# Reordering the first output block of a retention + MoE kernel: one chunk's casts ahead of two decays, transposes ahead of half units, weight sums and four down steps earlier

## The chip, the cores and the metric

The kernel runs on one core of a Trainium2 chip. A core has a matrix engine (PE in the profile, with its weight loads shown apart as PEld), a vector engine (DVE), a scalar engine (ACT), a general engine (POOL) and a sync engine (SP) that here only issues DMAs. Each engine takes its own instructions in order and waits on semaphores for the others. The metric is the device time of one execution in microseconds. Before the change it is 301.66 us, the median of three runs (300.08, 302.08 and 301.66 us).

## What is computed

Two operations, one behind the other. The first is a retention layer over 8 batches, 8 heads, 576 positions and 64 columns per head: scores of queries and keys, masked to the past and damped by a power of each head's gamma, times the values. Its result, brought to 4608 tokens by 512 columns, goes through a two-layer MLP with a hard-swish between the layers.

```
scores = scale * np.matmul(q, k.transpose(0, 1, 3, 2))
gamma = 1.0 - 2.0 ** (-5.0 - np.arange(H, dtype=np.float32))
Dmat = np.where(rel >= 0, gamma[:, None, None] ** rel[None, :, :], 0.0)
x = np.matmul(scores * Dmat[None], v)              # (B, H, S, D)
x = x.transpose(0, 2, 1, 3).reshape(B * S, H * D)  # 4608 x 512
h = x @ w_in                                       # 512 -> 2048
g = h * np.clip(h + 3.0, 0.0, 6.0) / 6.0
out = g @ w_out                                    # 2048 -> 512
```

The inputs and the output are fp32 in DRAM; the kernel's matrix products take fp16.

## The kernel before, in words

**Blocks and chunks.** The 4608 tokens are taken as nine blocks of 512. Block 0 holds the first 64 positions of all eight batches (the "heads" functions); block kb from 1 to 8 holds the last 512 positions of batch kb-1, in four chunks of 128 positions, numbered c = 4 kb to 4 kb + 3. So chunks 4 to 7 belong to block 1, 8 to 11 to block 2, and so on. A running state carries the past from chunk to chunk.

**Steps of a chunk.** Each step has a letter in the written-out plans:

- `c` (`casts`, line 182): keys to fp16 (ACT; POOL for chunks 7 to 9), for an even chunk the queries of two chunks, scaled, in two halves (`L192`, both on POOL, but for chunks 4 and 6 the second half on DVE), the values scaled (`L195`, POOL). It also issues the loads of a later chunk on SP.
- `t` (`transposes`, 198): products with an identity on PE into PSUM tiles `ptk` and `ptq`, copied out by ACT (`kT`) and DVE (`qT`), line 211.
- `a` (`scores`, 244) and `s` (`states`, 288): products of keys and queries, and of keys and values, into the two PSUM tiles `pa`; DVE multiplies the scores with the mask (`L267`).
- `u` (`add`, 311): DVE adds the new state (`L314`, and `L317` for the next chunk), POOL damps it (`L318`). `z` (`past`, 320): ACT casts the states to fp16 (`L324` to `L327`).
- `x` (`cross_over`, 347) and `i` (`inner`, 351): products of queries with states, and of scores with values, into the PSUM tiles `po`; `i` first has PE wait for the end of `x`. ACT copies `po` into the block's `xT` (`L370`).

**The MLP.** A unit (`U`, `up_steps`, 492) makes 128 of the 2048 hidden columns for 512 tokens: eight products, `ph`, then ACT's `u` (`L511`) and DVE's `g` (`L513`). A half unit pair (`up_two`, 526; written `L2` or `R2`, for the left or right 256 tokens) makes two such columns groups for half of the tokens with 16 products, one `L539` on ACT and one `L540` on DVE; an `L4` is two pairs. A down step (`D`, `down_plain`, 562) is one product of two halves with `w_out`, 64 steps for a block, into the PSUM tiles `pd`; ACT copies each finished `pd` out (`L574`). Blocks 2 to 8 use `down_strassen` (580), which needs eight sums of quarters of `w_out`, each 128x1024 in fp16 on DVE. `weight_sums` (662) only queues them; each `+1` in a plan emits the next of the queue (`side_sums`, 543, at `L545`). Their targets `ws1` to `ws4` hold other things at first: `ws1` the keys and `ws4` the values of block 0.

**The decays of block 0.** `head_states(c)` (`h` in the plan, 272) computes for c = 0 to 3 the state that the first 64 positions of batches c and c + 4 leave, in two PSUM tiles `pu`, and stores both times a power of gamma in `zh[c]` and `zh[c + 4]`: the first by DVE straight out of PSUM (`L283`), the second by an ACT copy (`L282`) and a POOL multiplication in place (`L284`). `zh[0]` is the past of chunk 4, the others serve later blocks.

**Order.** The order on PE, DVE, ACT, POOL and SP is the order in which the program emits the instructions: nothing rearranges them. It is written by hand as strings, one item a step, which `go` (710) reads from left to right. Three calls of `go` cover block 0's down steps, block 1 and the beginning of block 2; from there a loop with tables sets the order.

**Buffers.** All PSUM tiles but `pd` share a ring of six (`psum`, tag "pp", line 62): each new tile waits until the tile six places before it has been read out. `pd` has a ring of two of its own. Loads of keys and values have four buffers each, of queries two.

Of the kernel before, what the change touches and what calls it, by code (L numbers as in the profile page):

```python
# [16 lines left out]
ALU = mybir.AluOpType  # L17
# [4 lines left out]
def kernel(  # L22
# [9 lines left out]
    nc = tc.nc  # L32
    B, H, S, D = q.shape
# [7 lines left out]
    NCB = BLK // P  # L41
# [45 lines left out]
    zh = [const.tile([P, NP, D], FP32, name=f"zh{b}") for b in range(B)]  # L87
# [184 lines left out]
    def head_states(c):  # L272
        pu = [psum.tile([P, NP, D], FP32, tag="pp", name=f"pu{e}_{c}") for e in range(2)]
        todo = ([], [])
        for i in range(NP):
            for a in range(2):
                j, h2 = divmod(i + NP * a, 2)
                for e in range(2):
                    todo[e].append(mm(pu[e][rows(a), i], kn[rows(e), j, c, h2 * D:h2 * D + D],
                                      vh[rows(e), c, j, h2, :], start=True, stop=True))  # L280
        in_turn(todo)
        nc.scalar.copy(zh[c + NCB], pu[1])  # L282
        nc.vector.tensor_tensor(zh[c], pu[0], decay, ALU.mult)  # L283
        nc.gpsimd.tensor_tensor(zh[c + NCB], zh[c + NCB], decay, ALU.mult)  # L284

    zs, z16s, sums = {}, {}, {}

# [274 lines left out]
    def down_plain(kb):  # L562
        pieces = [range(4 * pc, 4 * pc + 4) for pc in range(4)]
        o = [out_tile(kb, m2) for m2 in range(2)]
        for m2 in range(2):
            pd = [psum.tile([P, DM], FP32, tag="st", bufs=2, name=f"pd{kb}_{2 * m2 + m}") for m in range(2)]
            for fcs in (pieces[0], pieces[2], pieces[1], pieces[3]):
                for m in range(2):
                    for fc in fcs:
                        hf, jq, jr = fc // JH, fc % JH // JQ, fc % JQ  # L570
                        product(pd[m], gt[kb, jq][0][:, hf, m2, jr, P * m:P * m + P], wout16[:, fc, :],
                                start=(fc == 0), stop=(fc == NFC - 1))
                        if fc == NFC - 1:
                            nc.scalar.copy(o[m2][:, m, :], pd[m])  # L574
                            if m:
                                kept.append((kb, m2, o[m2]))
                        yield
# [129 lines left out]
                {"c": cast, "t": lambda c: transposes(c, True, "kq" if c < PE_T else "k" if c < PE_K else ""), "a": scores, "s": states, "u": add, "z": past,  # L707
                 "x": cross_over, "i": inner, "k": keys_heads, "h": head_states, "o": lambda _: store(*kept.popleft())}[what](c)

    def go(plan, kb=None, down=None):  # L710


        units = dict(L=0, R=0, U=0)
        for item in plan.split():
            what, n = item[0], int(item[1:])
            if what == "D":
                for _ in range(n):
                    next(down, None)
            elif what in "LR":
                assert n % 2 == 0  # L720
                for _ in range(n // 2):
                    up_two(kb, units[what], "LR".index(what))
                    units[what] += 2
            elif what in units:
                for _ in range(n):
                    u = units[what] + (units["L"] if what == "U" else 0)
                    up_unit(kb, u, dict(L=0, R=1, U=None)[what])
                    units[what] += 1
            else:
                do([(what, n)])  # L730
        assert units["L"] == units["R"] and units["L"] + units["U"] == (0 if kb is None else NFC)
# [14 lines left out]
    with tc.manual_schedule(engines={ENG.PE, ENG.DVE, ENG.Pool, ENG.Activation, ENG.SP}):  # L746
        sp, act, pool = nc.sync, nc.scalar, nc.gpsimd
        on_act, on_dve = nc.scalar.copy, nc.vector.tensor_copy
        indices()
        for nm in ("k", "q"):  # L750
            landed = load_half(0, nm, 0, sp)
            keys = landed if nm == "k" else keys
            load_half(0, nm, 1, act)
        nc.scalar.activation(warm, half, ACTF.Exp)
        load_half(1, "q", 0, sp)
        load_half(1, "q", 1, act)
        for i in (2, 3):
            for e in range(2):
                load_half(i, "q", e, sp, keys)
        for i in (1, 2, 3):  # L760
            for e in range(2):
                load_half(i, "k", e, pool, None if i == 1 else keys)
            if i == 1:
                nc.gpsimd.memset(pick, 0.0)  # L764
        for i in range(NP):
            load_values(i)
        win_piece(0, 2)
        for n in (1, 2, 3):
            win_piece(n)
        wout = [wout_piece(pc) for pc in (0, 2, 1, 3)]  # L770
        distances()
        idle_products(5)
        mask_of_heads(0)
        cast_heads(0, "k", on_dve)
        picks()
        turn_heads(0, "k", on_act)
        mask_of_heads(1)
        idle_products(4)
        cast_heads(0, "q", on_dve)
        mask_of_heads(2)  # L780
        turn_heads(0, "q", on_act)
        cast_heads(1, "q", on_dve)
        turn_heads(1, "k", on_act)
        turn_heads(1, "q", on_act)
        cast_heads(2, "q", on_dve)
        scores_heads(0)
        mask_of_heads(3)
        idle_products(1)
        turn_heads(2, "k", on_act)
        turn_heads(2, "q", on_act)  # L790
        cast_heads(3, "q", on_dve)
        scores_heads(1)
        idle_products(1)
        turn_heads(3, "k", on_act)
        turn_heads(3, "q", on_act)
        scores_heads(2)
        values_heads(0, on_act)
        scores_heads(3)
        values_heads(1, on_act)
        inner_heads(0, on_act)  # L800
        values_heads(2, on_dve)
        inner_heads(1, on_dve)
        values_heads(3, on_act)
        inner_heads(2, on_dve)
        first = [up_steps(0, u) for u in range(4)]
        for dmc in range(3):
            for unit in first:
                next(unit)
            if dmc == 1:
                inner_heads(3, on_act)  # L810
        for unit in first:
            for _ in unit:
                pass
        decays()
        mask_of_chunk()
        decays_of_chunk()
        fetch(8, wout[0])
        for u in range(4, NFC):
            up_unit(0, u)
        weight_sums(3)  # L820
        weight_sums(1, 2, 4)
        down = down_plain(0)
        go("k0 D4 k1 D4 +1 k2 D4 +1 k3 D5 h0 h1 D4 h2 h3 c4 D7 t4 c5 D7 a4 s4 u4 D3 t5 D3 z4 x4 a5 s5 i4 u5 z5 c6 D7 "
           "x5 i5 D5 L2 t6 c7 L4 a6 s6 u6 L2 t7 z6 L2 x6 a7 s7 i6 u7 z7 D5 L2 c8 x7 i7 t8 D6 "
           "R4 c9 R2 a8 s8 u8 R2 t9 z8 R4 c10 x8 a9 s9 i8 u9 U1 z9 c11 t10 U3",
           1, down)
        down = down_plain(1)
        go("c12 D6 x9 a10 s10 i9 u10 z10 D2 t11 c13 +1 D7 x10 a11 s11 i10 u11 z11 c14 +2 D8 x11 D2 i11 t12 +1 D3 +1 D3 "
           "a12 s12 u12 t13 D2 c15 D2 z12 +1 D4 x12 a13 s13 i12 u13 z13 D1",
           down=down)  # L830
        go("U1 D3 t14 U1 D2 U1 U1 D2 x13 a14 s14 i13 u14 z14 o1 c16 U1 D2 U1 D2 t15 U1 D2 U1 D2 +1 U1 x14 a15 s15 i14 u15 z15 "
           "c17 D2 U1 D2 +1 U1 D2 +1 U1 D2 x15 +1 U1 i15 t16 c18 +1 U1 D2 t17 U1 U1",
           2, down)
        for kb in range(2, NB):
            for _ in down:
                pass
            plain = kb < FIRST
            down = down_plain(kb) if plain else down_strassen(kb)
            per = 4 if plain else 7
            table = FIRST_STEADY if kb == 2 else STEADY  # L840
            c = NCB * (kb + 2)
            owed = 0
            for u in range(NFC):
                if u == 0:
                    owed += per - 2
                    for _ in range(per - 2):
                        next(down, None)
                if kb + 1 < NB:
                    up_unit(kb + 1, u)
                else:  # L850
                    side_sums(1)
                owed -= per
                while owed < 0:
                    next(down, None)
                    owed += 1
                for w, i in table.get(u, []):
                    if w == "D":
                        for _ in range(i):
                            next(down, None)
                        owed += i  # L860
                    else:
                        do([(w, i if w == "+" else c + i)])
        for _ in down:
            pass
# [30 lines left out]
```

## Time and profile before

The profiled execution took 300.3 us, of which the profile's span is 298.6 us; its time lies 1.4 us under the median of the runs. The granted clock of PE is 1.00 throughout.

| | before |
|---|---|
| median of three runs | 301.66 us |
| profiled execution | 300.3 us |
| its span | 298.6 us |
| PE busy | 286.0 us (96%) |
| DVE busy | 215.6 us (72%) |
| ACT busy | 191.1 us (64%) |
| POOL busy | 134.0 us (45%) |
| DMA | 160 GB/s mean |

The times in a profile's lines are microseconds from the start of the span. In a timeline, a line gives start, length, engine, source line, operation, the tile written and the tiles read, the count, and in brackets how long the engine sat idle before it and what released it; an `L` number is a line of the kernel. A matmul's end is modelled and lies past the start of the next one, so the distance between starts tells better how long PE needed for a step than the lengths do. Waits of an engine that nobody waits for cost nothing.

### The profile page before, as it was taken

The page shows a single profiled execution, that of the slowest core. Times are in us where ns is not written, and L with a number is a line of the kernel's source. Part 1 is how long each engine was busy: PE and PEld are TensorE (multiplying, and loading weights), DVE is VectorE, ACT ScalarE, POOL GpSimd, SP SyncE. Part 2 cuts the span into 40 slices and gives each one's busy share as a digit, 9 for nine tenths or more (in the row PEclk, how much of TensorE's full clock was granted, in tenths as well). Part 3 has the DMA queues.
Part 4 walks back from the last instruction along what each step waited for, and adds up shares of the span by engine and source line. Part 5 has one row for each costly group of instructions (what it writes and reads, how often), then busy time and mean ns, then how long its engine had stood idle before and what let it go on. Part 6 is the DMA issues. An engine that isn't in the chain of part 4 may idle for free.

```text
span 298.6 us, 12625 instructions
## 1 busy us (share of the span) xinstructions
PE 286.0 (96%) x5574; PEld 221.2 (74%) x5574; DVE 215.6 (72%) x378; ACT 191.1 (64%) x345; POOL 134.0 (45%) x171
## 2 busy tenths in 40 slices
PE   4999989899999999999999999999999999999995
PEld 2676645778656667878987878878778978778894
DVE  7748554759897668788967797688769776647654
ACT  3748855678866796686676577657766574555420
POOL 8971074455861920729632962386247003100510
PEclk9999999999999999999999999999999999999999
DMA  7999999996999999996999999999906100200114
GB/s 166 151 182 213 233 239 221 232 221 121 164 214 162 207 240 195 186 234 195 218 239 218 172 199 214 148 180 242 149 4 143 74 4 32 102 10 2 72 72 141
DMA packets 119542, 47.86 MB, mean 160 GB/s; under 512 B 92352, under 2 KB 114880, under 8 KB 119488
## 3 DMA queue, kind: packets, MB, share of 16 engines
q1 hardware_dynamic: 114336, 41.56, 70.5%
q0 software_dynamic: 4720, 5.11, 10.5%
q8 instruction: 43, 0.70, 1.0%
q10 hardware_dynamic: 432, 0.39, 0.5%
q14 instruction: 11, 0.09, 0.1%
HBM read 36.70 MB, written 9.44 MB: 155 GB/s over the span
## 4 chain that ended last, share of the span: by engine, by line
PE 84%; POOL 5%; ACT 3%; DMA 3%; DVE 2%; issue 1%; POOLq 0%; ACTq 0%
PE ph L153 39%; PE pm L153 29%; PE pd L153 8%; PE po L232 4%; DMA win<-in_moe_w_in_dram 3%; PE pa L232 2%; POOL hv L440 1%; ACT u L539 1%; DVE g L540 1%; POOL hk L400 1%; PE pu L232 1%; POOL zh L284 1%; ACT kT L211 1%; POOL ws L764 1%; PE ptk L153 1%
## 5 line engine op out<-in xcount | busy, mean ns | idle before, releaser
L153 PE MATMUL ph<-xT,win 128*64 128x512 f16 (+1 forms) x1248 | 144.5, 364 | 0.7 <-DMA win<-in_moe_w_in_dram 0.4
L513 DVE SCALAR_TENSOR_TENSOR g<-u,ph 128x512 f16<-128x512 f32 x132 | 89.5, 685 | 47.7 <-ACT u L511 47.3
L511 ACT ACTIVATE u<-ph,half 128x512 f32<-128x512 f32 x132 | 90.2, 691 | 42.0 <-PE ph L153 39.9
L153 PEld LDWEIGHTS <-win 128*64 128x64 f16 x1248 | 84.2, 136 | 26.4 <-DMA win<-in_moe_w_in_dram 0.9
L153 PEld LDWEIGHTS <-g 128*64 128x64 f16 x928 | 51.8, 110 | 14.8 <-issue 0.6
L153 PEld LDWEIGHTS <-s 128*64 128x64 f16 x896 | 50.2, 110 | 8.1 <-issue 0.2
L318 POOL TENSOR_TENSOR z<-z,gpow 128x256 f32<-128x256 f32 x24 | 16.1, 673 | 70.7 <-DVE z L317 50.0
L153 PE MATMUL pm<-ws,s 128*64 128x256 f16 x672 | 45.4, 273 | 0.0
L195 POOL TENSOR_TENSOR v<-fv,dec 128x512 f16<-128x512 f32 x32 | 35.5, 1112 | 3.0 <-DMA fv<-in_v_dram 3.0
L370 ACT CAST xT<-po 128x256 f16<-128x256 f32 (+1 forms) x44 | 22.6, 585 | 21.4 <-PE po L232 21.4
L609 POOL TENSOR_TENSOR u<-u,p 128x512 f32<-128x512 f32 x7 | 8.9, 1273 | 60.1 <-ACT u L649 53.9
L192 POOL TENSOR_TENSOR q<-fq,dec 128x512 f16<-128x512 f32 x30 | 34.7, 1176 | 0.0
L153 PE MATMUL pd<-wout,g 128*64 128x512 f16 x256 | 33.6, 381 | 0.1
L153 PE MATMUL pm<-wout,g 128*64 128x256 f16 x448 | 31.6, 273 | 0.0
L267 DVE TENSOR_TENSOR a<-pa,mask 128x256 f16<-128x256 f32 (+1 forms) x44 | 21.9, 539 | 8.3 <-PE pa L232 5.1
L545 DVE TENSOR_TENSOR s<-g 128x1024 f16<-128x1024 f16 x28 | 19.3, 692 | 0.2
L324 ACT CAST z<-z 128x512 f16<-128x512 f32 x24 | 14.9, 622 | 5.8 <-DVE z L314 5.5
L188 ACT CAST k<-fk 128x512 f16<-128x512 f32 x29 | 18.0, 622 | 0.1
L153 PE MATMUL pm<-ws,g 128*64 128x256 f16 x224 | 16.7, 274 | 0.0
L153 PE MATMUL pm<-wout,s 128*64 128x256 f16 x224 | 16.4, 273 | 0.1
L232 PE MATMUL po<-qT,z 64*64 64x64 f16 x512 | 12.6, 198 | 2.0 <-ACT z L327 0.9
L232 PEld LDWEIGHTS <-z 64*64 64x64 f16 x512 | 8.0, 105 | 8.0 <-ACT z L324 2.2
(110 smaller groups left out, 293.6 us busy)
## 6 DMA issues: line engine op xcount, KB each, us to landing
fk<-in_k_dram SPq DMA_DIRECT2D x32, 256.0 KB, 4.7
fq<-in_q_dram SPq DMA_DIRECT2D x16, 512.0 KB, 5.9
fv<-in_v_dram SPq DMA_DIRECT2D x32, 256.0 KB, 5.5
out_dram<-o SPq DMA_DIRECT2D x14, 512.0 KB, 3.7
wout<-in_moe_w_out_dram POOLq DMA_DIRECT2D x4, 512.0 KB, 17.8
out_dram<-o SPq DMA_DIRECT2D x7, 256.0 KB, 4.0
win<-in_moe_w_in_dram POOLq DMA_DIRECT2D x3, 512.0 KB, 11.3
hq<-in_q_dram SPq DMA_DIRECT2D x6, 128.0 KB, 4.3
```

Of the source, the lines that this page charges most:

```text
L153: nc.tensor.matmul(out[r], lhs[:, r], rhs, skip_group_check=True, **flags)
L188: (nc.gpsimd.tensor_copy if c in K_POOL else nc.scalar.copy)(by_head(k16), in_rows(st[c]["fk"]))
L192: (nc.vector if e and c in Q_DVE else nc.gpsimd).tensor_tensor(by_head(q16[:, e]), in_rows(st[c]["fq"][:, :, e, :]), in_rows(dd[:, 2 + e, ...
L195: nc.gpsimd.tensor_tensor(v16, st[c]["fv"], dd[:, 1, H:2 * H, :], ALU.mult)
L232: return lambda: nc.tensor.matmul(*args, skip_group_check=True, **flags)
L267: nc.vector.tensor_tensor(a16[:, a, 0:n].rearrange("p x i q -> p (x i) q"), pa[a].rearrange("p x i q -> p (x i) q"), m, ALU.mult)
L318: nc.gpsimd.tensor_tensor(new, new, decay, ALU.mult)
L324: nc.scalar.copy(z16, zs[c])
L370: nc.scalar.copy(xt[:, s], po[s].rearrange("p x n (e r) -> p x n e r", e=2))
L511: nc.scalar.activation(uu[:, 0:n], ph[:, 0:n], ACTF.Relu, bias=half, scale=1.0 / 6.0)
L513: nc.vector.scalar_tensor_tensor(out=g[:, hf, ths, jr, :], in0=by_half(uu), scalar=1.0, in1=by_half(ph), op0=ALU.min, op1=ALU.mult)
L545: nc.vector.tensor_tensor(*pend.popleft())
```

## The change

Four pieces, all between block 0's down steps and the last chunk of block 3.

1. In `head_states`, for c = 0 and 1, DVE multiplies the second state too, straight out of PSUM; the ACT copy and the POOL multiplication stay for c = 2 and 3 only. In the plan `c4` moves ahead of `h2 h3`, so that chunk 4's casts stand ahead of two of the decays on ACT, POOL and DVE.
2. `t6` moves ahead of the first half units (`L2` goes behind it, into a later `L4`), and down steps are placed differently: one more ahead of `t4`, two more ahead of `x4`, two between `x5` and `i5`, one between `x7` and `i7`, fewer behind.
3. Of the six sums that stood in the second plan, four are emitted in the first, between `c5` and `c6`.
4. Block 1's down steps get a generator `ahead` from the start, and the new letter `E` takes four of them ahead of the first full unit `U1`; the second plan starts with two down steps where it had six.

On SP the order is the same as before, on PE no product is added or dropped, DVE gets two instructions more, ACT and POOL two fewer.

```
     def head_states(c):
...
-        nc.scalar.copy(zh[c + NCB], pu[1])
         nc.vector.tensor_tensor(zh[c], pu[0], decay, ALU.mult)
-        nc.gpsimd.tensor_tensor(zh[c + NCB], zh[c + NCB], decay, ALU.mult)
+        if c < 2:
+            nc.vector.tensor_tensor(zh[c + NCB], pu[1], decay, ALU.mult)
+        else:
+            nc.scalar.copy(zh[c + NCB], pu[1])
+            nc.gpsimd.tensor_tensor(zh[c + NCB], zh[c + NCB], decay, ALU.mult)
...
-    def go(plan, kb=None, down=None):
+    def go(plan, kb=None, down=None, ahead=None):
...
-            if what == "D":
+            if what in "DE":
                 for _ in range(n):
-                    next(down, None)
+                    next(down if what == "D" else ahead, None)
...
-        down = down_plain(0)
-        go("k0 D4 k1 D4 +1 k2 D4 +1 k3 D5 h0 h1 D4 h2 h3 c4 D7 t4 c5 D7 a4 s4 u4 D3 t5 D3 z4 x4 a5 s5 i4 u5 z5 c6 D7 "
-           "x5 i5 D5 L2 t6 c7 L4 a6 s6 u6 L2 t7 z6 L2 x6 a7 s7 i6 u7 z7 D5 L2 c8 x7 i7 t8 D6 "
-           "R4 c9 R2 a8 s8 u8 R2 t9 z8 R4 c10 x8 a9 s9 i8 u9 U1 z9 c11 t10 U3",
-           1, down)
-        down = down_plain(1)
-        go("c12 D6 x9 a10 s10 i9 u10 z10 D2 t11 c13 +1 D7 x10 a11 s11 i10 u11 z11 c14 +2 D8 x11 D2 i11 t12 +1 D3 +1 D3 "
-           "a12 s12 u12 t13 D2 c15 D2 z12 +1 D4 x12 a13 s13 i12 u13 z13 D1",
+        down, ahead = down_plain(0), down_plain(1)
+        go("k0 D4 k1 D4 +1 k2 D4 +1 k3 D5 h0 h1 D4 c4 h2 h3 D8 t4 c5 +1 D7 a4 s4 u4 +1 D3 t5 D5 z4 x4 a5 s5 i4 u5 z5 +1 c6 +1 D7 "
+           "x5 D2 i5 D4 t6 c7 L4 a6 s6 u6 L2 t7 z6 L4 x6 a7 s7 i6 u7 z7 D3 L2 c8 x7 D1 i7 t8 D3 "
+           "R4 c9 R2 a8 s8 u8 R2 t9 z8 R4 c10 x8 a9 s9 i8 u9 E4 U1 z9 c11 t10 U3",
+           1, down, ahead)
+        down = ahead
+        go("c12 D2 x9 a10 s10 i9 u10 z10 D2 t11 c13 +1 D7 x10 a11 s11 i10 u11 z11 c14 +1 D8 x11 D2 i11 t12 D6 "
+           "a12 s12 u12 t13 D2 c15 D2 z12 D4 x12 a13 s13 i12 u13 z13 D1",
            down=down)
```

## Prediction

> **What bounds the kernel.** I read the busy times first, then the same by stretches of the span, then in the stretches where PE is not full its timeline, its waits and the chain that ended last. PE has 96% of the span:
>
> ```profile
> PE 286.0 (96%) x5574; PEld 221.2 (74%) x5574; DVE 215.6 (72%) x378; ACT 191.1 (64%) x345; POOL 134.0 (45%) x171
> ```
>
> By stretches (start:end and length, then busy time of PE, its weight loads, DVE, ACT and POOL, the granted clock, the DMA share and GB/s):
>
> ```profile
> 33.00:44.80 11.80, 10.35 (x200) 5.91 (x197) 6.27 (x11) 7.91 (x18) 5.77 (x7) 1.00 1.03 242
> 44.80:52.00 7.20, 6.49 (x180) 3.80 (x180) 3.62 (x9) 3.85 (x9) 2.87 (x4) 1.00 1.11 216
> 52.00:64.30 12.30, 11.03 (x292) 9.11 (x290) 8.77 (x17) 8.63 (x16) 8.02 (x10) 1.00 1.00 222
> ...
> 113.00:282.00 169.00, 168.92 (x3320) 138.20 (x3318) 127.59 (x208) 109.83 (x188) 69.53 (x65) 1.00 0.73 142
> ```
>
> From 113 to 282 us PE is busy 168.92 of 169.00 us, so whatever PE gains ahead of it moves the end one for one; nothing there is touched. The change lies where PE is short of work, 33 to 64 us. The chain of 40 to 44 us shows why at the worst place:
>
> ```profile
> 39.44 0.80 POOL zh L284 x2
> ...
> 40.55 1.05 POOL zh L284
> 41.60 1.01 POOL q L192
> 42.61 0.04 issue
> 42.66 0.64 PE ptq L153 x16
> ```
>
> Four decays run on POOL, then chunk 4's query cast, and PE's transposes wait for that cast. PE's timeline, by starts:
>
> ```profile
> 39.28 1.70 PE L153 MATMUL pd<-wout,g 128*64 128x512 f16 x14
> 40.81 0.39 PE L153 MATMUL ptk<-ident,k 128*64 128x128 f16 x8
> 42.66 0.64 PE L153 MATMUL ptq<-ident,q 128*64 128x128 f16 x16 [1.46 <-POOL q L192]
> ...
> 47.46 0.26 PE L232 MATMUL po<-qT,z 64*64 64x64 f16 x8 [0.64 <-ACT z L327]
> ...
> 55.48 0.32 PE L232 MATMUL pa<-qT,kT 64*64 64x64 f16 x16 [0.34 <-DVE qT L211]
> ...
> 58.73 0.26 PE L232 MATMUL po<-qT,z 64*64 64x64 f16 x8 [0.68 <-DVE g L540]
> ```
>
> A down step costs 0.216 us (seven, 14 products, take 39.28 to 40.79), a half unit pair 0.87 (51.68 to 52.55), a key transpose 0.23 (46.01 less 45.78), a query transpose 0.44 (52.78 to 53.21). Start to start less this work leaves these stalls: 0.12 at `h2`; 1.63 at `t4` (42.66 less 41.03); 0.80 at `x4`; 0.20 at `x5`; 0.35 between `x5` and `i5`; 0.50 at `a6` (54.97 to 55.48); 0.85 at `x6`; 0.35 at `x7`; 0.25 between `x7` and `i7`; and 0.10 changing over at `a4`. Sum **5.15 us**. Behind it, `U1` at 71.68 loses 0.43 (`i8` ends at 71.25) and `x12` at 88.57 loses 0.78.
>
> **The change, step by step.** PE's work is the same, so the sum is the stalls of before less those left. I carry PE, DVE, ACT and POOL through the new order with the durations above.
>
> *Chunk 4's casts.* The decays of `h0` and `h1` go to DVE: two more at 0.41 (four took 1.64), so DVE is done with them at 38.38 + 1.64 = 40.02, as before with its own four. The second `pu` of `h0` is now freed at 39.20, and the ring of six makes `h3` wait for it: 0.15. The two ACT copies saved (0.33 each) lay beside idle ACT and give nothing. The query cast cannot start before its load: DVE's half began at 40.20, released by the load. So POOL starts 1.4 earlier than 41.57, at 40.2. But now both halves start together, with the next decays of DVE behind its half. Alone a POOL half is 1.04; the longest in the trace is 1.49, and DVE's two took 0.68 and 0.93. The casts end between 41.2 and 41.85, against 42.61. With the eighth down step PE reaches `ptq` at 41.37 (39.42 + 8 x 0.216 + 0.22). The second half of `ptq` also needs the ring place of `h2`, freed when DVE has done that decay, 0.41 behind its cast. Stall left: 0.15 to 0.9; I take 0.55, nearer the contended rows. Left at this place 0.12 + 0.15 + 0.55 = 0.82 of 1.75.
>
> *Down steps at `x4`.* The cast of the state was late because `t5`'s copy and two casts (0.58, 0.41, 0.41) follow on ACT. `D5` covers 0.43 more; 0.1 is left of 0.80.
>
> *Sums.* Four sums of 0.69 come into DVE between 43 and 51 us, where DVE idled 0.82, 1.27 and 3.28 us: they fit, alone. They read SBUF beside POOL's casts, and there the trace shows them dear (DVE's lines, then POOL's):
>
> ```profile
> 81.83 2.68 DVE L545 TENSOR_TENSOR ws<-wout,ws 128x1024 f16<-128x1024 f16 x2
> 84.43 1.53 DVE L545 TENSOR_TENSOR ws<-wout 128x1024 f16<-128x1024 f16 x1
> ```
>
> ```profile
> 81.47 2.49 POOL L192 TENSOR_TENSOR q<-fq,dec 128x512 f16<-128x512 f32 x2
> 83.92 1.49 POOL L195 TENSOR_TENSOR v<-fv,dec 128x512 f16<-128x512 f32 x1
> ```
>
> A sum beside POOL takes 1.34 to 1.53 and POOL's cast 1.25 to 1.49. So each may hold DVE 0.69 to 1.53. The first ends ahead of `a4`'s masks or 0.6 into them, which `D3 t5 D5` (1.96) covers; the second and POOL's 0.99 damping put `x5` off: I leave 0.2 there, between 0 and 0.4. The third and fourth stand around chunk 6's query cast: DVE's half would be done by 50.1, POOL's between 49.7 and 51.2, PE at `ptq` at 50.7: 0 to 0.55 left, I take 0.3. Their old places, 81.8 to 88, were no gain: `x12` there waits for ACT's row of `kT`, `o`, `k` and two `z` casts behind `t13`, whose order stays. I leave its 0.78.
>
> The Trainium skill, "SBUF — State Buffer", "Who interferes with whom", says that a vector instruction with two SBUF inputs and a GpSimd one that reads SBUF exclude each other, and the later to start waits for the whole of the other. The 1.53 beside 1.49 agrees; this speaks against pieces 1 and 3, as it makes the two halves of chunk 4's cast follow one another. By that rule at its worst (0.9, 0.4 and 0.55 left at `t4`, `x5` and `t6`) the gain of the sum below would be 2.2 instead of 3.0; without any contention (0.15, 0 and 0) it would be 3.9.
>
> *`D2` and `D1`* between `x` and `i` cover the change of PSUM writer that cost 0.35 and 0.25; nothing of it is left, as 0.43 is over 0.35 and 0.22 near 0.25.
>
> *`t6` ahead of `L4`.* The copies of `qT` (1.28 on DVE) then run beside 1.74 of half units, so `a6` loses its 0.50. `L4` in place of `L2` ahead of `x6` gives ACT and DVE 0.87 more, and the 0.85 falls to 0.15 (the third `g` frees `a7`'s place). But the two pairs put their `u` and `g` ahead of chunk 7's masks. From the end of the first `L4` (taken as 0): its last `u` and `g` end at 1.66, masks and states of chunk 6 at 3.1, three more `g` at 5.2, masks and `L314` of chunk 7 at 6.25, ACT's cast at 6.85; PE has work for 5.95. So `x7` stalls **0.9** where it stalled 0.35. Here between 0.3 and 1.5, as one `g` (0.61) more or less comes ahead.
>
> *`E4`* covers `U1`'s 0.43 with 0.86 of work. What it takes away are four down steps ahead of `x9`, whose state is cast at 74.0, 3.3 us early, and whose ring places are free by 77.53; `x10` then stands about 0.1 ahead of its state. Cost 0.1. No wait is added on SP.
>
> *Loads.* Chunks 4 to 7 land from 40 to 51 us; POOL's waits there are for DVE. From 44 to 64 us DMA moves 216 to 222 GB/s, near the most of any slice (242), but from 70 to 77 us it rests (0.55 of its time, one idle gap of SP from 67 to 72), so chunks from 12 on have room to move forward with PE.
>
> **Sum.** Left: 0.82, 0.1 (`x4`), 0.2, 0, 0.3 (`t6`), 0, 0.15, 0.9, 0, with 0.03 of changing over = 2.5. Gain 5.15 - 2.5 + 0.43 - 0.1 = **3.0 us**, 300.3 - 3.0 = 297.3 for an execution like the profiled one, 298.7 counted from the median of 301.66. The runs spread over both, so I say **297.9**. A change under about 1% (3.0 us) can hardly be told from none here.
>
> **Rivals.**
> - *Every stall goes:* the chain to `x7` is shorter than my sum and the casts do not collide. For it: DVE idles 7.4 us between 41 and 54 us. Gain 5.15 + 0.43 = 5.6, less the load's bound (0.15): 5.4, 2.4 more than the forecast, so 295.5. Against: the load at 40.2 and three `g` ahead of chunk 7. Chance 0.12.
> - *A new wait takes the gain:* PE comes early to `t4`, `t6` and `x7` and finds the upper ends: 0.35, 0.25 and 0.6 more, `x5` 0.2 more, 1.4 in all, and up to 1 us at loads or at the ring. Gain 0.6 to 1.6, some 1.9 less than the forecast: 299.8. That a plan's pieces give each other's gain back (or that the order does nothing at all) ends here too. Chance 0.18.
> - *Slower: DVE starves beside POOL.* If DVE's half of chunk 4's cast had to wait for POOL's whole row `q v zh zh v` (3 x 1.04 + 2 x 0.61 = 4.3), it would end at 45.2 and `ptq`, after the decay behind, at 45.7: 3.9 over my 41.8. The same at chunk 6 (row `z q v k v`, 4.3, against 1.4 allowed) costs 2.9 more: 297.3 + 6.8 = 304.1. It decides once DVE loses to more than about two POOL instructions in a row. Against: from 81.47 to 84.5 both engines moved in turn. Chance 0.10, a fifth of it within 1%.
>
> **Chances and range.** Forecast 0.60, two thirds of it over 3.0 us, as fewer collisions than I took are likelier than more once the four sums fall into DVE's idle time. Faster by over 1%: 0.40 + 0.12 = 0.52. Within: 0.20 + 0.18 + 0.02 = 0.40. Slower: 0.08. The forecast's own range is 296.4 to 299.4; 8 in 10 reaches from the first rival to most of the second: 295.3 to 300.8.
>
> **What would show it.** POOL's `q` starting near 40.2 and PE's `ptq` near 41.5 to 42; the wait of `ptq` for POOL under 0.9; sums of 0.7 to 1.5 us between 43 and 52; no wait at `a6`; `x7` waiting for ACT about 0.9; PE's first right half unit at 61 to 62 in place of 64.32; `U1` without a wait. I am wrong if `ptq` starts past 42.5, if `x7`'s wait is over 1.5, or if loads show among PE's or ACT's waits ahead of 70 us.

## The result, and the profile after

Over fourteen executions each, the changed kernel takes 299.23 us in the median (298.64 to 301.09) and the kernel before 300.9 us (299.33 to 303.17). The ratio is 0.9949, with a 95% interval of 0.9926 to 0.9973: about 1.5 us gained, between 0.8 and 2.2 us (the medians alone lie 1.7 apart). I had forecast 3.0 us and 297.9 us. The direction was right, and the size is half of what I said, so the gain fell among the cases within 1%, not into the likeliest one. That 299.23 still lies inside the forecast's range (296.4 to 299.4), 0.2 us from its end, owes something to luck: single executions of one kernel differ by more, and the gain itself was mis-sized by half.

The profiled execution of the changed kernel took 301.1 us, the longest of its fourteen, with a span of 299.4 us against 298.6 before. From line 284 on, a line of the kernel before has a number higher by 3 in the changed kernel (`L324`, `L327`, `L370`, `L540` and `L545` are now `L327`, `L330`, `L373`, `L543` and `L548`); `decays_pool` keeps the numbers of before. The busy times by stretches after (start:end and length; busy time of PE, its loads, DVE, ACT, POOL; clock; DMA share; GB/s):

```profile
33.00:44.80 11.80, 11.63 (x204) 6.84 (x200) 7.62 (x16) 8.22 (x18) 3.41 (x4) 1.00 0.93 218
44.80:52.00 7.20, 6.98 (x182) 3.75 (x180) 6.39 (x13) 3.86 (x10) 4.65 (x5) 1.00 1.00 225
52.00:64.30 12.30, 11.48 (x298) 9.51 (x296) 9.48 (x18) 8.62 (x17) 9.15 (x11) 1.00 1.08 240
113.00:282.00 169.00, 167.67 (x3302) 136.62 (x3298) 127.09 (x207) 108.59 (x185) 68.70 (x65) 1.00 0.75 141
```

In the three stretches that the change touches, PE's idle time fell from 1.45, 0.71 and 1.27 us to 0.17, 0.22 and 0.82 (roughly the same work: this execution is there about 1 us later). But from 113 to 282 us, where nothing was changed, PE stood idle 1.33 us against 0.08 before. The waits of PE after (line, what it waited for, us in total, times, longest) name two of the losses outside the change:

```profile
PE ph L153 <- DMA win<-in_moe_w_in_dram: 1.5, 2, 1.0
PE po L232 <- issue: 1.0, 1, 1.0
```

The first is at the start, where the loads of `w_in` landed late (0.4 us before); the second is at 153 us and is released by nothing that the profile shows. So the two spans can't be set against each other. I compare marks instead: **L**, where DVE starts its half of chunk 4's query cast (released by the load); chunk 4's `ptq` on PE; **B**, the first right half unit of block 1; **C**, block 2's first full unit. PE does the same work between L and C in both kernels. Before, L to C is 49.30 us, in a second execution 49.23; after, 47.49 and 47.49. That is a gain of **1.8 us**, and it agrees with the timed 0.8 to 2.2. The two ends, DVE's line at L and PE's at C, before and then after:

```profile
40.20 0.93 DVE L192 TENSOR_TENSOR q<-fq,dec 128x512 f16<-128x512 f32 x1 [0.18 <-DMA fq<-in_q_dram]
...
89.50 1.03 PE L153 MATMUL ph<-xT,win 128*64 128x512 f16 x8
```

```profile
41.25 0.69 DVE L192 TENSOR_TENSOR q<-fq,dec 128x512 f16<-128x512 f32 x1 [0.30 <-DMA fq<-in_q_dram]
...
88.74 1.03 PE L153 MATMUL ph<-xT,win 128*64 128x512 f16 x8
```

Counting from L takes the landing of the load as given. L lies 2.66 and 2.63 us behind the first `pu` products in the two profiles of before, 2.49 and 3.07 in the two of after, and 1.76 to 4.37 in the experiments below. Whether the change itself moves the load, so few executions can't tell.

The remaining 0.8 us that the profiled span is longer is a head 1.05 longer and a tail behind C 1.56 longer (210.66 against 209.10), less this gain.

The chain after, at the place where four decays and the cast had stood on POOL:

```profile
31.80 9.42 DMA fq<-in_q_dram
...
41.39 1.46 POOL q L192
```

The decays are gone from it: ahead of the cast now stands chunk 4's query load. PE's timeline after:

```profile
42.89 0.64 PE L153 MATMUL ptq<-ident,q 128*64 128x128 f16 x16 [0.17 <-POOL q L192]
...
46.24 1.25 PE L153 MATMUL pd<-wout,g 128*64 128x512 f16 x10
47.70 0.25 PE L232 MATMUL po<-qT,z 64*64 64x64 f16 x8 [0.21 <-ACT z L330]
...
50.07 0.26 PE L232 MATMUL po<-qT,z 64*64 64x64 f16 x8
50.26 0.62 PE L153 MATMUL pd<-wout,g 128*64 128x512 f16 x4
50.81 0.25 PE L232 MATMUL po<-qT,z 64*64 64x64 f16 x8
50.90 0.30 PE L232 MATMUL po<-a,v 64*64 64x64 f16 x16
...
52.94 1.91 PE L153 MATMUL ph<-xT,win 128*64 128x256 f16 x32
54.79 0.32 PE L232 MATMUL pa<-qT,kT 64*64 64x64 f16 x16
...
59.67 1.26 PE L153 MATMUL ph<-xT,win 128*64 128x256 f16 x16
61.65 0.25 PE L232 MATMUL po<-qT,z 64*64 64x64 f16 x8 [0.72 <-ACT z L327]
...
63.83 2.35 PE L153 MATMUL ph<-xT,win 128*64 128x256 f16 x40
```

The stall at `ptq` is nearly gone, `a6` (54.79) has lost its wait, and `x7` (61.65) is now the dear place: the pair ahead of it needs 0.87, so PE stood 1.11 us from 60.54 on.

### The profile page after: what moved, and what is told of

It is laid out like the page before. It is cut to its first block, busy times and chain, and to the rows that moved or that the text cites. A ratio compares the mean times of both kernels' runs of the same rounds, so it can differ in the third digit from the quotient of the medians.

```text
span 299.4 us, 12624 instructions
## 1 busy us (share of the span) xinstructions
PE 287.2 (96%) x5574; PEld 219.8 (73%) x5574; DVE 216.0 (72%) x380; ACT 190.5 (64%) x343; POOL 133.9 (45%) x169
## 4 chain that ended last, share of the span: by engine, by line
PE 77%; DMA 10%; POOL 6%; ACT 3%; DVE 2%; issue 1%; SPq 0%; POOLq 0%; ACTq 0%
PE ph L153 36%; PE pm L153 29%; DMA wout<-in_moe_w_out_dram 5%; PE pd L153 4%; PE po L232 3%; DMA fq<-in_q_dram 3%; PE pa L232 2%; DMA fv<-in_v_dram 2%; POOL hv L443 1%; POOL hk L403 1%; POOL win L679 1%; PE pu L232 1%; POOL q L192 1%; ACT z L327 1%; ACT kT L211 1%
## 5 line engine op out<-in xcount | busy, mean ns | idle before, releaser
L153 PEld LDWEIGHTS <-win 128*64 128x64 f16 x1248 | 83.1, 136 | 28.4 <-DMA win<-in_moe_w_in_dram 2.1
L153 PEld LDWEIGHTS <-g 128*64 128x64 f16 x928 | 50.6, 110 | 15.5 <-issue 0.4
L153 PEld LDWEIGHTS <-s 128*64 128x64 f16 x896 | 51.0, 110 | 8.2 <-issue 1.1
L153 PE MATMUL pm<-ws,s 128*64 128x256 f16 x672 | 46.1, 273 | 0.2 <-issue 0.2
L192 POOL TENSOR_TENSOR q<-fq,dec 128x512 f16<-128x512 f32 x30 | 35.6, 1204 | 17.2 <-DMA fq<-in_q_dram 17.2
L195 POOL TENSOR_TENSOR v<-fv,dec 128x512 f16<-128x512 f32 x32 | 36.2, 1134 | 2.6 <-PE ph L153 2.6
L373 ACT CAST xT<-po 128x256 f16<-128x256 f32 (+1 forms) x44 | 22.6, 585 | 21.4 <-PE po L232 21.4
L153 PE MATMUL pd<-wout,g 128*64 128x512 f16 x256 | 34.2, 382 | 0.1
L153 PE MATMUL pm<-wout,g 128*64 128x256 f16 x448 | 30.8, 273 | 0.0
L548 DVE TENSOR_TENSOR s<-g 128x1024 f16<-128x1024 f16 x28 | 19.4, 694 | 0.2
L327 ACT CAST z<-z 128x512 f16<-128x512 f32 x24 | 14.9, 620 | 7.0 <-DVE z L317 6.6
```

The costliest lines, as they stand in the source:

```text
L153: nc.tensor.matmul(out[r], lhs[:, r], rhs, skip_group_check=True, **flags)
L192: (nc.vector if e and c in Q_DVE else nc.gpsimd).tensor_tensor(by_head(q16[:, e]), in_rows(st[c]["fq"][:, :, e, :]), in_rows(dd[:, 2 + e, ...
L195: nc.gpsimd.tensor_tensor(v16, st[c]["fv"], dd[:, 1, H:2 * H, :], ALU.mult)
L327: nc.scalar.copy(z16, zs[c])
L373: nc.scalar.copy(xt[:, s], po[s].rearrange("p x n (e r) -> p x n e r", e=2))
L548: nc.vector.tensor_tensor(*pend.popleft())
```

## The experiments

All marks in microseconds. The kernel before has one down step (0.22) fewer ahead of `ptq` and one more behind it; the table counts it ahead in every run, so 0.22 is taken from `ptq` to B and the gain at `ptq` reads 1.04 for 0.82. At `i8`, in some executions, PE stood 0.1 to 0.55 us by the distance of the starts (where the profile names a releaser, it is "issue"); this is taken out of B to C, and 0.72 inside `x5` out of `casts_alone`.

| kernel | L to `ptq` | `ptq` to B | B to C |
|---|---|---|---|
| before, two executions | 2.46, 2.48 (+0.22) | 21.44, 21.34 | 25.18, 25.19 |
| after, two executions | 1.64, 1.65 | 20.94, 20.92 | 24.91, 24.92 |
| `casts_alone` | 1.65 (+0.22) | 21.44 | 25.20 |
| `sums_back` | 1.66 | 20.67 | 24.92 |
| `no_ahead` | 1.65 | 20.93 | 25.19 |
| `units_back` | 1.65 | 21.39 | 24.91 |
| `no_split` | 1.65 | 20.95 | 24.90 |
| `four_ahead_x7` | 1.95 | 20.93 | 24.96 |
| `decays_pool` | 1.65 | 22.60 | 24.90 |
| `pair_after_z7` | 1.65 | 21.04 | 24.94 |
| `z12_early` | 1.95 | 20.91 | 24.72 |
| `casts6_early` | 1.65 | 21.59 | 24.55 |

Marks of kernels with the same order between two marks agree to 0.1 (most to 0.05), while single times of one kernel lie up to 4 us apart. So the verdicts below go by marks, and by times only where many executions were made. Each experiment but `casts_alone` and `casts6_early` is a single execution. The first four expectations count from A, the first `pu` products, and so take in how late the load lands. By those marks two of them look like misses: in `units_back` the load came 3.76 behind A, and `casts_alone` takes 26.89 from A to B and 52.09 from A to C, no less than before (26.78 and 51.96). The later expectations count from L.

**`casts_alone`: the first piece alone, in the kernel before.** `head_states` as after, and

```
-h0 h1 D4 h2 h3 c4 D7 t4
+h0 h1 D4 c4 h2 h3 D7 t4
```

> The kernel before with piece 1 alone: chunk 4's casts ahead of h2 and h3, and DVE taking both decays for the first two chunks; plans otherwise as before. Marks are read from PE's timeline: A is the start of block 0's first state products (pu), B the first right half unit of block 1, C block 2's first full unit. Before: A to B 26.78, A to C 51.96 us; after: 25.08 and 49.99. Theory: the casts alone are worth most of the change, the wait of 1.63 at ptq falls to 0.4 to 0.6 and nothing later takes it back: A to B 25.6 to 25.9, A to C 50.7 to 51.1, time about 0.3 to 0.4% under before. Rival: the next wait (the state cast ahead of x4, 0.80) takes it: A to B 26.3 or more.

Ten executions took 300.48 us in the median against 301.63 of the kernel before: ratio 0.9959, 0.9925 to 0.9992, so about 1.2 us (0.2 to 2.3). PE's timeline:

```profile
41.95 0.64 PE L153 MATMUL ptq<-ident,q 128*64 128x128 f16 x16 [0.32 <-POOL q L192]
...
46.76 0.25 PE L232 MATMUL po<-qT,z 64*64 64x64 f16 x8 [0.64 <-ACT z L330]
...
50.04 0.50 PE L232 MATMUL po<-qT,z 64*64 64x64 f16 x9 [0.66 <-issue]
```

`ptq` comes 1.65 behind the load, 0.8 earlier than before, and nothing of this is given back up to C but for the wait named "issue" at 50 us. In this one profile that wait (0.72) and a load 0.21 later behind A take the whole 0.8; that the gain is real rests on the ten times and on the same 1.65 in nine other runs. `x4` stays 4.81 behind `ptq`, as after (42.89 to 47.70) and before (42.66 to 47.46): that distance is set by the copies and casts behind `ptq`, not by PE's work.

**`sums_back`: the four sums back in the second plan.**

```
-c5 +1 D7 a4 s4 u4 +1 D3 t5 D5 z4 x4 a5 s5 i4 u5 z5 +1 c6 +1 D7
+c5 D7 a4 s4 u4 D3 t5 D5 z4 x4 a5 s5 i4 u5 z5 c6 D7
...
-c14 +1 D8 x11 D2 i11 t12 D6 a12 s12 u12 t13 D2 c15 D2 z12 D4 x12
+c14 +2 D8 x11 D2 i11 t12 +1 D3 +1 D3 a12 s12 u12 t13 D2 c15 D2 z12 +1 D4 x12
```

> The kernel after with the four sums of w_out back at their old places in the second plan. Theory that their place is neutral: A to B 24.8 to 25.1 (25.08 with them), A to C within 0.2 of 49.99. Rival, that beside POOL's casts they cost what the prediction allowed at x5, t6 and a4 (0.5 to 0.8): A to B 24.3 to 24.6, and POOL's chunk 6 query cast at 1.04 to 1.2 in place of 1.49.

`ptq` to B is 0.26 shorter without the sums, and B to C is the same. So at their new place the sums cost 0.26, and leaving the old place gained nothing. POOL's timeline after, then DVE's after, then POOL's in `sums_back`:

```profile
50.93 1.49 POOL L192 TENSOR_TENSOR q<-fq,dec 128x512 f16<-128x512 f32 x1
```

```profile
50.41 1.10 DVE L192 TENSOR_TENSOR q<-fq,dec 128x512 f16<-128x512 f32 x1
51.44 1.52 DVE L548 TENSOR_TENSOR ws<-wout 128x1024 f16<-128x1024 f16 x1
```

```profile
50.68 1.04 POOL L192 TENSOR_TENSOR q<-fq,dec 128x512 f16<-128x512 f32 x1
```

After, the third sum puts DVE's half of chunk 6's cast beside POOL's half, and they take 1.10 and 1.49; in `sums_back` DVE's half (0.68) is done before POOL's starts, and POOL's takes 1.04. The sum that meets POOL's casts takes 1.52, where two others take 0.68. The exclusion that the prediction cited from the Trainium skill ("SBUF — State Buffer", "Who interferes with whom") fits these numbers; at this place it cost PE 0.26, within the 0 to 0.55 that I had allowed at `t6`, and less than the 0.5 to 0.8 of the rival.

**`no_ahead`: no down steps of block 1 ahead of `U1`.** `u9 U1` for `u9 E4 U1`, `c12 D6 x9` for `c12 D2 x9`.

> The kernel after with E4 taken out and the second plan starting with D6 again. Theory: the wait of U1 for its PSUM place comes back (0.43) and the 0.28 between x10 and a11 that after shows goes away, so A to C is 50.1 to 50.4 (49.99 with E4). Rival, that U1's wait had gone by the other pieces already: A to C 49.6 to 49.8.

B to C is 25.19 against 24.91: `E4` is worth 0.28. From the starts, 0.27: B to `U1` shortens by 0.44 when the four steps are not counted (7.36 before, 7.78 less 0.86 after), and `U1` to C lengthens by 0.17 (17.82 before, 17.13 and the 0.86 after).

**`units_back`: the transposes of chunk 6 behind the first pair again.**

```
-x5 D2 i5 D4 t6 c7 L4 a6 s6 u6 L2 t7 z6 L4 x6
+x5 D2 i5 D4 L2 t6 c7 L4 a6 s6 u6 L2 t7 z6 L2 x6
```

> The kernel after with the first two half units ahead of t6 again and two in place of four ahead of x6; down steps and sums as in after. Theory: moving t6 only shifted the wait, from a6 and x6 (0.50 and 0.85 before) to x7 (0.35 before, 1.1 after): A to B 25.0 to 25.4 and x7 waits 0.3 to 0.6. Rival, that the move of t6 is worth what the prediction gave it (a6 and x6 1.2, x7 0.55 back, so 0.65 net): A to B 25.6 to 25.9.

`ptq` to B is 21.39: the move is worth 0.45. Two waits of the profile before are back in PE's timeline, the first two here:

```profile
55.08 0.32 PE L232 MATMUL pa<-qT,kT 64*64 64x64 f16 x16 [0.34 <-DVE qT L211]
...
58.32 0.26 PE L232 MATMUL po<-qT,z 64*64 64x64 f16 x8 [0.68 <-DVE g L543]
...
61.28 0.26 PE L232 MATMUL po<-qT,z 64*64 64x64 f16 x8 [0.40 <-ACT z L327]
```

By the distance of starts PE stands 0.58 at `a6`, 0.85 at `x6` and 0.78 at `x7` (61.28 less 60.50), and not at chunk 6's `ptq`. After, it is 0.11, 0.31 with `a7` and `s7`, 1.11, and 0.23 at `ptq`. So of the 1.0 that the move gains at `a6` and `x6`, 0.56 comes back at `ptq` and `x7`.

**`after_again` and `before_again`: both kernels once more.**

> The kernel after, once more, to separate the change from what differs between executions. Theory: what sets the stage is the landing of chunk 4's query load (L, the start of DVE's half of the cast): ptq starts 1.65 us behind it as in the first execution (42.89 less 41.25), and from ptq to the first right half unit (B) it takes 20.94 and from B to C 24.91, each within 0.1, wherever A lies. Rival, that the order itself is unstable: ptq to B differs by 0.4 or more.

> The kernel before, once more. Theory: ptq starts 2.46 us behind L (42.66 less 40.20), ptq to B takes 21.66 (with one more down step of 0.22 in it than after) and B to C 25.18, each within 0.1. Rival: they move by 0.4 or more, and the comparison of two single profiles says little.

Their marks are in the table and repeat the first ones to 0.1. The span was 297.0 us after and 299.7 before, the other way round from the first pair of profiles. The "issue" waits were elsewhere and of other sizes: 0.33 at 150.8 us after, 0.34 at 129.5 and 0.60 at 153.5 before. Both kernels have them, so nothing here ties them to the change.

**`no_split`: no down steps between `x` and `i`.** `x5 i5 D6 t6` for `x5 D2 i5 D4 t6`, `x7 i7 t8 D4` for `x7 D1 i7 t8 D3`.

> The kernel after with the two down steps between x5 and i5 put behind i5, and the one between x7 and i7 behind t8. Theory: filling the change of PSUM writer with down steps saved little, since each change between 64-wide and 512-wide products costs about 0.1 itself: ptq to B 21.0 to 21.2 (20.94 with the split). The prediction's count, that they hide 0.35 and 0.25: 21.4 to 21.6.

Its timeline:

```profile
49.03 0.58 PE L232 MATMUL po<-qT,z 64*64 64x64 f16 x16
49.44 0.30 PE L232 MATMUL po<-a,v 64*64 64x64 f16 x16
...
60.60 0.58 PE L232 MATMUL po<-qT,z 64*64 64x64 f16 x16 [0.71 <-ACT z L327]
61.01 0.30 PE L232 MATMUL po<-a,v 64*64 64x64 f16 x16
```

Without the steps `x` and the wait for its end take 0.41 in both places. After, they take 0.83 with two steps (50.07 to 50.90) and 0.61 with one (61.65 to 62.26); less the steps' own 0.43 and 0.22 that is 0.40 and 0.39. The steps hide nothing: what is saved at the wait is lost in going over from the 64x64 products to 512 columns and back. `ptq` to B is 20.95, the same.

**`four_ahead_x7`: the wait of `x7` filled.** `D3 L2 c8 D4 x7 i7 t8` for `D3 L2 c8 x7 D1 i7 t8 D3`.

> The kernel after with the down steps that stood behind x7 and t8 (one and three) put ahead of x7. Theory that x7's wait of 1.1 is a chain of ACT and DVE from the first L4 on which PE's filling does not lengthen: 0.86 of work fits into it and one split goes, ptq to B 19.9 to 20.1. Rival, that the chain hangs on PE (more steps ahead push u and g of the last pair back): 20.6 or more.

```profile
59.70 1.09 PE L153 MATMUL pd<-wout,g 128*64 128x512 f16 x8
60.71 0.58 PE L232 MATMUL po<-qT,z 64*64 64x64 f16 x16
...
62.84 1.42 PE L153 MATMUL ph<-xT,win 128*64 128x256 f16 x22 [0.63 <-ACT xT L373]
```

`x7` does not wait any more, and the right half units wait 0.63 for ACT's `xT` instead: `ptq` to B is 20.93, unchanged, against the 19.9 to 20.1 of my theory. The row from chunk 7's state (`L327`) over `x7`, `i7` and `xT` to the right half units sets B, wherever PE's spare work is put.

**`pair_after_z7`: one pair fewer ahead of chunk 7's masks.**

```
-L2 t7 z6 L4 x6 a7 s7 i6 u7 z7 D3 L2 c8 x7 D1 i7 t8 D3
+L2 t7 z6 D3 L2 x6 a7 s7 i6 u7 z7 L4 c8 x7 i7 t8 D4
```

> The kernel after with one half unit pair taken from ahead of x6 to behind z7 and D3 in its place, no split at x7, and four down steps behind t8. Theory: the chain that sets the end of this stage is on DVE and ACT, three g ahead of chunk 7's masks, then states, cast, x7, i7, the copy of po to xT, which the right half units need; one g less ahead of the masks makes it 0.6 shorter: ptq to B 20.2 to 20.5 (20.93 with it). Rival, that it hangs on PE's order alone: 20.8 to 21.1, as filling x7's wait gave nothing.

```profile
57.47 0.33 PE L153 MATMUL ph<-xT,win 128*64 128x256 f16 x2
58.54 1.86 PE L153 MATMUL ph<-xT,win 128*64 128x256 f16 x30 [0.74 <-ACT xT L373]
60.33 0.58 PE L232 MATMUL po<-qT,z 64*64 64x64 f16 x16
```

`x7` finds its state ready, but the pair ahead of it waits 0.74 for a copy of ACT. `ptq` to B is 21.04, no better (0.1 is what two executions of one kernel differ by). The place of the pairs is no lever either.

**`decays_pool`: the first piece without DVE's decays.** `head_states` as before (copy on ACT, decay on POOL for every c), `c4` still ahead of `h2 h3`.

> The kernel after with the decays as before, the second state of every chunk by ACT's copy and POOL, and only the order of c4 kept. W is the landing of w_out's last piece (DVE's second sum), L that of chunk 4's query load. Theory: POOL is done with two decays before L, so the change of engine gave nothing and cost h3's wait behind DVE: ptq at L+1.65 as with it, and h3's products start 0.3 to 0.5 earlier against W. Rival, that POOL's two decays still stand in the cast's way: ptq at L+1.9 or more.

`ptq` again comes 1.65 behind the load. But in this execution the load itself was late, 41.51 us, which is 4.36 behind the first `pu` products (1.76 to 3.8 in the others), so POOL had time for its two decays:

```profile
38.43 1.18 POOL L284 TENSOR_TENSOR zh<-zh,gpow 128x256 f32<-128x256 f32 x2 [14.79 <-ACT zh L282]
```

They end at 39.61, 2.46 behind the first `pu` products, where the load came 2.45 or more behind them in all but two of the other runs with `c4` in this place. From these times, the gain of the first piece comes from where `c4` stands, and the two instructions moved to DVE would give something only where the load is early (1.76); no run shows that case. PE stood 2.14 us. PE's timeline, then three stretches (columns as above):

```profile
43.16 0.96 PE L153 MATMUL ptq<-ident,q 128*64 128x128 f16 x16 [2.14 <-POOL q L192]
43.91 3.07 PE L153 MATMUL pd<-wout,g 128*64 128x512 f16 x14
46.91 0.32 PE L232 MATMUL pa<-qT,kT 64*64 64x64 f16 x16
```

```profile
39.90:43.30 3.40, 1.26 (x24) 0.71 (x20) 1.36 (x3) 1.13 (x3) 1.65 (x2) 1.00 0.58 123
43.31:46.72 3.41, 3.41 (x30) 1.70 (x26) 2.06 (x3) 1.14 (x2) 3.39 (x4) 0.50 0.99 254
46.73:50.10 3.37, 3.16 (x112) 1.85 (x113) 2.11 (x5) 1.20 (x3) 0.99 (x1) 1.00 1.03 216
```

Behind that wait the granted clock stood at 0.50 for 3.41 us, then at 1.00 again; `ptq` took 0.75 to the next start in place of 0.47, and the seven steps behind it 3.00 in place of 1.61. These 1.67 us are the whole of what `ptq` to B is longer (22.60 less 20.93).

**`z12_early`: chunk 12's casts of states ahead of `c15` on ACT.** `t13 D2 z12 c15 D6 x12` for `t13 D2 c15 D2 z12 D4 x12`.

> The kernel after with z12 ahead of c15, so that ACT casts the state ahead of chunk 15's keys. The prediction's reading, that x12's 0.78 hangs on ACT's row behind t13: B to C 24.3 to 24.5 (24.92 in after), x12 waits 0.3 or less. Rival, that DVE's masks and states set it: 24.8 to 25.0.

```profile
85.30 2.23 PE L153 MATMUL pd<-wout,g 128*64 128x512 f16 x16
87.46 0.26 PE L232 MATMUL po<-qT,z 64*64 64x64 f16 x8
87.54 0.30 PE L232 MATMUL pa<-qT,kT 64*64 64x64 f16 x16
87.89 0.32 PE L232 MATMUL pa<-v,k 64*64 64x64 f16 x16
```

After, the same eight steps also begin at 85.30 and `x12` comes at 87.81. It now comes 0.35 earlier, but `s13` then stands 0.22 behind `a13` (87.54 to 87.89; 87.89 to 88.02 after). From `E4`'s start to C the kernel takes 17.83 us where eight runs with the old order take 18.01 or 18.02: 0.19 gained of the 0.78. What `s13` waits for, the profile does not name. In `casts6_early`, which has the same order of `z12`, `s13` does not stand, and E4 to C is 0.36 shorter than after, all that `x12` gained.

**`casts6_early`: chunk 6's casts a step earlier, with `z12` early and two sums back.**

```
-z4 x4 a5 s5 i4 u5 z5 +1 c6 +1 D7 x5 D2 i5 D4 t6 c7 L4
+z4 x4 c6 a5 s5 i4 u5 z5 D7 t6 x5 D2 i5 D4 c7 L4
...
-c14 +1 D8 x11 D2 i11 t12 D6
+c14 +2 D8 x11 D2 i11 t12 +1 D6
...
-t13 D2 c15 D2 z12 D4 x12
+t13 D2 z12 c15 D6 x12
```

> The kernel after with chunk 6's casts ahead of a5, t6 ahead of x5, the two sums that stood around chunk 6's cast moved to the second plan, and z12 ahead of c15. Theory: from ptq to B the stage is one chain, chunk 6's cast, its transposes, the first L4, then u and g, masks and states of chunks 6 and 7 on ACT and DVE up to the copy of po that the right half units read; filling PE's wait at its end (three runs) gave nothing, beginning it earlier does: ptq to B 19.9 to 20.3 (20.93 in after, 20.67 with the sums back), x7's wait 0.2 to 0.5 in place of 1.1; time against before about 0.8 to 1.0% less. Rival, that the stage is held at the pace at which loads land or at the ring of six: 20.6 to 21.0, 0.5 to 0.6% less.

The theory was that an earlier `t6` shortens the row down to chunk 7. It does not: `ptq` to B is 21.59, 0.65 longer. DVE's timeline, then PE's:

```profile
48.21 0.69 DVE L192 TENSOR_TENSOR q<-fq,dec 128x512 f16<-128x512 f32 x1 [1.58 <-DMA fq<-in_q_dram]
48.82 0.75 DVE L267 TENSOR_TENSOR a<-pa,mask 128x256 f16<-128x256 f32 x2
```

```profile
49.85 0.64 PE L153 MATMUL ptq<-ident,q 128*64 128x128 f16 x16 [0.54 <-POOL q L192]
50.60 0.25 PE L232 MATMUL po<-qT,z 64*64 64x64 f16 x8
```

Chunk 6's queries land at 48.2. DVE waited 1.58 for them with chunk 5's masks queued behind, so chunk 5's state and `x5` came late. From `E4` to C it takes 17.66, 0.36 less than after. Its twelve executions took 299.01 us against 301.51 before: 0.9921, 0.9897 to 0.9945. This interval overlaps the change's own, and its L to C (47.8) is no shorter, so it is not shown to be better; that its time came out near the 0.8% of my theory says nothing for that theory, which its marks contradict. A kernel with `sums_back` and `z12_early` together should have the shortest marks, by estimate 47.5 - 0.26 - 0.19 = 47.0; it was not run.

## Why the prediction was right in direction and half in size

The terms, as forecast and as the marks give them:

| place | forecast gain | measured gain |
|---|---|---|
| up to `ptq` (decays, casts, eighth step) | 0.93 | 1.04 |
| `ptq` to B | 1.72 | 0.46 |
| `E4`, B to C | 0.33 | 0.27 |
| sum | 3.0 | 1.8 |

**Chunk 4's casts: right.** I left 0.82 of 1.75; the gain was 1.04 where I had 0.93. The bound I named, the load and both halves of the cast beside each other, decides: POOL's half takes 1.45 (forecast 1.04 to 1.49), and `ptq` stands 1.65 behind the load in ten runs with `c4` in this place. In the two others (1.95) the load came only 1.76 behind the first `pu` products and PE's own work was the limit. The wait for `h3` did come up in some runs (0.82 in `units_back`, where DVE stood behind the load of `w_out`), but `ptq` waited for its own load anyway. DVE's decays I counted as part of this piece; in the one run without them POOL's did as well, with a late load.

**`E4`: right.** Gain and price were both near what was said (0.44 and 0.17, for 0.43 and 0.10).

**`ptq` to B: the step that failed.** The stalls left there are 2.9 by the starts, not 1.68. Place by place:

- `x4`: 0.38, where I left 0.1. Here I mis-subtracted: 0.80 less the 0.43 of two more steps is 0.37. `x4` is pinned 4.8 behind `ptq`, as three kernels show.
- *`D2` and `D1` between `x` and `i`:* 0.45 left, where I left nothing. `no_split` shows that they save nothing. I took the gap for a pure wait that any work fills, and charged nothing for going over to other products and back. This is the largest single miss.
- `a6` 0.11 for 0, and 0.11 with a further 0.20 at `a7` and `s7` for 0.15 at `x6`. The mechanism was right (`units_back` brings both waits back); only these remainders were not in my sum.
- `x7`: 1.11 for 0.9, inside its bounds. I had its row right: the cast of chunk 7's state ends 6.9 behind the first `L4` (54.68 to 61.60; forecast 6.85). So the move of `t6` was worth 0.45 net, and not more, because this row and not PE sets B.
- The sums: I had left 0.2 at `x5` and 0.3 at `t6`; the starts show 0.20 and 0.23, and `sums_back` puts the whole cost at 0.26. The hit at `x5` is luck: the same 0.2 stands there before and in `sums_back` (49.62 to 49.83), so the sums do not cause it.
- Changing over at `a4`: 0.10 as before, where the sum had 0.03 without a reason.

The misses (0.28, 0.45, 0.11, 0.16, 0.21, 0.07 at `a4`, less 0.07 at `t6`) are 1.21 of the 1.26 between 1.72 and 0.46; the rest is within what single starts tell.

**The rivals.** "A new wait takes the gain" came nearer in size (0.6 to 1.6; timed 1.5, by the marks 1.8), but by other means: the upper end was not met at `t4` or `t6`, and at `x7` by 0.2 only. "Every stall goes" is out because of the load and of chunk 7's row. DVE did not starve beside POOL: its half of the cast took 0.69 at chunk 4 and 1.10 at chunk 6. `x12`'s 0.78 stayed, as left in the sum.

**The signs.** I had written that I am wrong if `ptq` starts past 42.5. It started at 42.89, because this execution's head was 1.05 later (`w_in`'s loads), and in the second one at 41.57. A mark counted from the start of the span was a poor sign; counted from the load it would have been right. For the same reason my sign that no load may show among PE's waits ahead of 70 us failed on `w_in`, outside the change. The first right half unit came at 63.83, and at 62.49 in the second, against a forecast of 61 to 62.

## What to carry to other kernels

When stalls follow one another along one row (a state handed from chunk to chunk), removing one mostly moves the next: find the row that sets the last mark, here chunk 7's state, and count only what shortens that row. Work put into a short wait pays only if it costs nothing to switch to it; test one such place before counting on all. Where effects are a few tenths of a microsecond, compare distances between marks inside the stage, counted from the load that releases it, and not spans.

## What the runs showed of the hardware that I had not expected

- **PE's unexplained waits.** PE stands 0.2 to 1.3 us at places that change from execution to execution, with "issue" as releaser: none in the profiles of before, `sums_back`, `no_ahead` and `four_ahead_x7`, 1.02 at 153 us after, 1.26 at 152.75 in `casts6_early`. Several fall near the same places (128 to 130 us, 151 to 155 us, and `i8` near 70). What causes them is open. From C to the end, where all these kernels run the same order on PE, the time lies between 208.96 and 210.66, as much as the change itself gains.
- **A wait that costs the clock.** 2.14 us without work at `ptq` were followed by 3.41 us at a granted clock of 0.50 and 1.67 us more for the next work (`decays_pool`); the wait of 1.46 us of the kernel before at the same place cost no clock. The Trainium skill, "TensorE: Matmul & The Clock Gate", Part 1, describes a gate that halves the clock after at least one idle window of about 3.4 us, with windows that run on whatever the kernel does. The halving and the 3.41 us agree; the wait does not, as it was shorter, and in the 3.40 us up to the drop PE was busy for 1.26. That a shorter wait can already do it is what this run shows; one run does not tell where the limit lies.
